# Moving the attention output's normalizing product from GpSimd to VectorE in a planned transformer block

## The chip, the cores and the metric

The kernel runs on one core of one Trainium2 chip. A core has five engines, each with its own in-order queue: TensorE (PE; its weight loads are shown apart as PEld), VectorE (DVE), ScalarE (ACT), GpSimd (POOL) and SyncE (SP), which here issues all DMA transfers. The metric is the device time of one execution in microseconds (us), as a median of runs.

## The reference

One transformer block in bf16 on 2048 tokens of width 640: a pre-norm attention with 32 heads of width 20, then a gated MLP of inner width 1728, each with a residual.

```python
h = x + _A_ref(_layernorm(x, axis=-1), A_wqkv, A_wo)
h2 = h + _B_ref(_layernorm(h, axis=-1), B_w_gate, B_w_up, B_w_down)

# _A_ref
qkv = transpose((x @ wqkv).reshape(B, S, 3, H, Dh), 2, 0, 3, 1, 4)
scores = jnp.einsum("bhqd,bhkd->bhqk", q, k) * (Dh ** -0.5)
p = _softmax(scores, axis=-1)
o = jnp.einsum("bhqk,bhkd->bhqd", p, v)
return transpose(o, 0, 2, 1, 3).reshape(B, S, D) @ wo

# _B_ref
h = gelu(x @ w_gate) * (x @ w_up)
return h @ w_down
```

## The kernel before

**Tiling.** The 2048 queries are cut into eight chunks (`SIZES` = 512, five of 256, two of 128). Heads go in eight groups of four, the four heads of a group lying at partitions 0, 32, 64 and 96. A slot is one chunk's work on as many groups as make 512 columns (a 256-query chunk has two groups per slot); there are 32 slots. Within a slot a tile is 128 x 512 scores of one head.

**Exponentials.** Score matmuls (L972) write PSUM banks 0 to 4. ACT takes them as units of alternately three and two tiles (1536 and 1024 columns) and writes bf16 weights to the ring `pts`, whose last part lies in `rege`. Some tiles (`D_SLOT`: three steps of four tiles in most slots) VectorE does instead: one instruction for each tile (L885) makes a 16-bit integer pattern from PSUM, and four value rounds of 128 x 2048 (`TERMS`, L896) turn a pattern into four bf16 terms of an exponential's approximation. Each round's result feeds its own value matmuls. `SUMS` says in how many cases of a slot two rounds are added first (a pair sum, L902), which saves PE one pass. `D_FIRST` and `D_SPAN` say over how many units of a slot these tiles are spread.

**Value matmuls and the end of a slot.** Value matmuls (L923) add up in bank 6. A column of ones in the values gives each query's sum too. When a slot is done, VectorE copies bank 6 to `osb` (L1045). For all chunks but the last `spread` (from L1019) then brings the sums, which lie in one partition for each head, to 16 columns on 128 partitions through DRAM (`sums`, then `rc`), GpSimd makes reciprocals of them with ten small instructions, and three more DMA steps (`rsums`, then four `bsum`) repeat them over 32 partitions for each head. One product, `on16 = osb * bsum`, 128 x 512 (L1034), normalizes the output, and four DMAs (`attn`) store it. When a chunk's slots are through, `post` (from L1097) runs the output projection, the second norm and the MLP of that chunk as background work beside the next chunk's slots; the norm's reciprocal root is a row of small GpSimd instructions. The last chunk's `post` is the tail.

**Order.** Nothing is ordered by hand. Every operation is given to `Sched.op` with an engine, a planned duration, a priority (lower goes first) and what it reads and writes. `schedule` plays the operations through with these durations and fixes the order of every engine's queue; `emit` writes the queues with semaphore waits. A result is taken to be ready its duration and a latency after its start: `lat`, or else the engine's entry in `DRAIN` (0.085 us for VectorE). Score matmuls are due `QK_LEAD` before ACT is expected to be free (L233). PE goes on with operations of its present tiling mode until another one has been ready for longer than `PE_AGE` (L168). Where PE would be idle too much, `schedule` puts in filler matmuls, groups of four small ones (`zer`) or one wide one on `kt_all`.

**Other names.** `XN_DVE` lists the token tiles whose transposed copy VectorE makes in the prologue, the others being ACT's. `P_EPI` is priority 2. All DMAs are issued by SP. Operations recorded through the helper `I` carry line 391 in the profile, so there the tile names tell them apart.

Of the kernel before, what the change touches and what calls it, by code (L numbers as in the profile page):

```python
# [8 lines left out]
ALU = mybir.AluOpType  # L9
# [9 lines left out]
DRAIN = {"pe": 0.165, "act": 0.115, "dve": 0.085, "pool": 0.05, "sp": 0.0}  # L19
WARM_WIN, WARM_MIN = 3.4, 0.5  # L20
PAD_WIN, PAD_MIN = 3.4, 0.42
QK_LEAD = .62
PE_AGE = 2.5
SD_AGE = 0.6


# [22 lines left out]
class Sched:  # L49
# [13 lines left out]
    def op(self, eng, fns, dur, prio, reads=(), writes=(), acq=(), rel=(), after=(), sem=None, lat=None, mode=None, util=0.0, rows=()):  # L63
        if eng == "dve" and rel and prio > self.ev:
            prio = self.ev
        o = Op()
        o.i = len(self.ops)
        o.eng, o.dur, o.lat, o.sem = eng, dur, DRAIN[eng] if lat is None else lat, sem
        o.util = util
        o.mode = mode  # L70
        o.rows = rows
        o.tag = writes[0] if writes else None
        o.fns = fns if isinstance(fns, list) else [fns]
        o.prio = (prio, o.i)
        deps = set(after)
        for r in reads:
            if r in self.lw:
                deps.add(self.lw[r])
        for w in writes:
            if w in self.lw:  # L80
                deps.add(self.lw[w])
            deps.update(self.rd.get(w, ()))
        for r in reads:
            self.rd.setdefault(r, []).append(o.i)
        for w in writes:
            self.lw[w] = o.i
            self.rd[w] = []
        deps.discard(o.i)
        o.deps = deps
        o.acq = list(acq)  # L90
        o.rel = list(rel)
        o.succ = []
        o.ready = 0.0
        self.ops.append(o)
        return o.i

    def schedule(self):
# [25 lines left out]
        while done < total:  # L123
# [4 lines left out]
            for e in ENGINES:  # L128
# [8 lines left out]
                while ready[e]:  # L137
# [28 lines left out]
                    if chosen is None:  # L166
                        chosen, banks = o, got
                        if e != "pe" or p[0] < 1 or o.mode == mode[e] or t - o.ready > PE_AGE:  # L168
                            break
# [62 lines left out]
                if e == "act":  # L232
                    due = t + o.dur + (0.905 if o.dur > 1.2 else 1.332) - QK_LEAD if o.mode == "exp" else None  # L233
                if o.util:
# [111 lines left out]
PV_QUADS = 2  # L346
PR, PR2 = 12, 4
D_SLOT = (0,) + (3,) * 27 + (2,) * 2 + (1,) * 2
SUMS = (0,) + (1,) * 30 + (0,)
HOP = 2.6  # L350
RECIP_MAGIC = float(0x7EF311C3)
COL = 256
VN = 6
SIX = ()
D_FIRST, D_SPAN = 0, 17
TANH_FROM = 768
GELU_A = 2.0 * 0.7978845608028654
GELU_B = 4.0 * GELU_A * 0.044715
# [2 lines left out]
P_EV = 1.8  # L361
P_QK, P_PV, P_TAIL, P_PRO, P_EPI, P_LN, P_BG = 0, 1, 1.2, 1.5, 2, 2.5, 3
P_KQ = 3
V_ACT = (0, 1)
XN_DVE = (13, 14, 15)
V0 = 0
LATE = (0, 1, 2, 3, 4)

# [1 line left out]
def bass_sequential_preLN__mha_block__glu_gated_geglu__prompt_kernel(  # L370
# [12 lines left out]
    with ExitStack() as es:  # L383
        sc = Sched(nc)
        op = sc.op

        def sb(name, shape, dt=BF16):
            return es.enter_context(nc.sbuf_tensor(name, shape, dt))

        def I(method, *args, **kwargs):  # L390
            return lambda eng: getattr(eng, method)(*args, **kwargs)  # L391
# [8 lines left out]
        def c_dve(n, rate=1.0625):  # L400
            return 0.061 + n * rate * 1e-3
# [23 lines left out]
        osb = sb("osb", [128, 2, 512], FP32)  # L425
        rc = sb("rc", [128, 2, 16], FP32)
        rn = sb("rn", [128, 2, 16], FP32)
        bsum = sb("bsum", [128, 512], FP32)
        on16 = sb("on16", [128, 512])
# [67 lines left out]
        def bank(b, n=512):  # L497
            return PS[:, 512 * b.b:512 * b.b + n]
# [5 lines left out]
        POOL = "pool"  # L504

        def cst(fn, key, n=128):
# [7 lines left out]
           reads=["zer"], writes=["qf1"])  # L514
        op("act", I("activation", f32(qt_all[:, 2, :, :]), zer[:, 0:2].bitcast(FP32).to_broadcast([128, 2048]), ACT.Copy), 1.8, P_QK,
           reads=["zer"], writes=["qf2"])
# [138 lines left out]
        for t0 in (0, 4, 8, 12):  # L655
# [6 lines left out]
            for t in range(t0, t0 + 4):  # L662
                e_ops.append(ln_apply("dve", x_sb[:, t, :], xn_p[:, t % 4, :], ("xnp", t % 4), t, [f"x{t // 4}"], P_PRO))
                transposes(xn_p[:, t % 4, :], [("xnp", t % 4)], xnT[:, :, t * 128:(t + 1) * 128], ("xnT", t),
                           ALLB, P_PRO, "dve" if t in XN_DVE else "act")
                e_ops.append(len(sc.ops) - 2)
# [24 lines left out]
        def dma(dst, src, key, reads, sem, lat, prio, issue=DMA_ISSUE, keep=True):  # L691
            i = op("sp", I("dma_start", dst, src), issue, prio, reads=reads, writes=[key], sem=sem, lat=lat)
            if keep:
                w_readers.append(i)
            return i
# [133 lines left out]
        for s_, (c, gs) in enumerate(slots):  # L829
            mine = list(dict.fromkeys(x[1:3] for x in tiles if x[0] == s_))  # L830
            n = D_SLOT[s_]
            d_kb[s_] = [mine[(2 * i + 1) * len(mine) // (2 * n)] for i in range(n)]
            k = min(SUMS[s_], 2 * n)
            d_sums[s_] = [(i + 1) * k // max(n, 1) - i * k // max(n, 1) for i in range(n)]
# [43 lines left out]
        def d_exp(b, tile, prio):  # L878
            c = slots[tile[0]][0]
            qb = CHUNKS[c][0] // 512  # L880
            e = min(qb, 2)
            h = len(d_raw)
            v, vk = d_v[e][d_n[e] % len(d_v[e])]
            aft = tuple(e_ops) + (tuple(last_qk[0]) if qb else ()) + (tuple(last_qk[1]) if qb > 1 else ())
            d_ops.append(op("dve", lambda eng: eng.tensor_scalar(v[:, 512 * h:512 * h + 512], bank(b), EXP_MUL, -32000.0,  # L885
                                                                 ALU.mult, ALU.max), c_dve(512), P_QK,
                            reads=[("SD", tile)], writes=[vk], rel=[b], after=aft))
            d_raw.append(tile)
            if h < 3:
                return  # L890
            d_n[e] += 1
            pairs = d_sums[tile[0]].pop(0)
            for i, off in enumerate(TERMS):
                a, ak = d_a[e][d_t[e] % len(d_a[e])]
                d_t[e] += 1
                d_ops.append(op("dve", I("tensor_scalar", a, v, 0.25, off, ALU.mult, ALU.add), 0.6, prio,  # L896
                                reads=[vk], writes=[ak], after=aft))
                if i // 2 < pairs:
                    if i % 2 == 0:
                        m, mk = a, ak  # L900
                        continue
                    d_ops.append(op("dve", I("tensor_tensor", m.bitcast(BF16), m.bitcast(BF16), a.bitcast(BF16), ALU.add), 1.13, prio,  # L902
                                    reads=[mk, ak], writes=[mk], after=aft))
                    a, ak = m, mk
                pv_op([[(a[:, 512 * k:512 * k + 512].bitcast(BF16), ak, x) for k, x in enumerate(d_raw)]], tile[0])
            d_raw.clear()
# [41 lines left out]
        def unit(u):  # L948
# [53 lines left out]
            if xd:  # L1002
                d_exp(bd, xd, P_EPI)
# [15 lines left out]
        def spread(s, c, gs, nq):  # L1019
            n = len(gs)  # L1020
            h = lambda dst, src, reads, key, sem, issue: dma(dst, src, key, reads, sem + str(s), HOP, P_EPI, issue, keep=False)
            h(sdr[s], osb[DH:128:32, s, :], [("osb", s)], ("sdr", s), "sa", 0.1)
            h(rc[:, s, :], sdr[s].rearrange("j (a b) -> (j a) b", b=16), [("sdr", s)], ("rc", s), "sb", 0.4)
            x, y, z = rc[:, s, :], rn[:, 0, :], rn[:, 1, :]
            d = lambda fn, r, w: op(POOL, fn, 0.285, P_EPI, reads=r, writes=w)
            d(I("tensor_scalar", y.bitcast(I32), x.bitcast(I32), -1.0, RECIP_MAGIC, ALU.mult, ALU.add), [("rc", s)], ["ry"])
            for i in range(3):
                d(I("tensor_tensor", z, x, y, ALU.mult), [("rc", s), "ry"], ["rz"])
                d(I("tensor_scalar", z, z, -1.0, 2.0, ALU.mult, ALU.add), ["rz"], ["rz"])
                d(I("tensor_tensor", x if i == 2 else y, y, z, ALU.mult), ["ry", "rz"], [("rc", s) if i == 2 else "ry"])  # L1030
            h(rdr[s].rearrange("j (a b) -> (j a) b", b=16), rc[:, s, :], [("rc", s)], ("rdr", s), "sc", 0.4)
            for j in range(4):
                h(bsum[32 * j:32 * j + 32, :], rdr[s, j].partition_broadcast(32), [("rdr", s)], ("bs", j), "sd", 0.36)
            op(POOL, I("tensor_tensor", on16[:], osb[:, s, :], bsum[:], ALU.mult), 1.4, P_EPI,  # L1034
               reads=[("osb", s)] + [("bs", j) for j in range(4)], writes=["on16"])
            for j in range(4):
                h(adr[c][gs[0]:gs[0] + n, j].rearrange("g e s -> e g s"),
                  on16[32 * j:32 * j + DH, :].rearrange("p (g s) -> p g s", g=n), ["on16"], ("adr", c, gs[0], j), "se", 0.36)

        def epilogue(s_, bk):  # L1040
# [6 lines left out]
            if c < len(CHUNKS) - 1:  # L1047
                spread(s, c, gs, nq)
                return
# [195 lines left out]
        for kt in range(NT):  # L1245
            proj_v(kt, 0, (6, 7), P_EPI if kt < VN else P_BG, "act" if kt in V_ACT else "dve")
        
        ui = 0
        for s_, (c, gs) in enumerate(slots):
            if c == 0:  # L1250
                g = s_
                if g + 1 in STEP:
                    t, (g0, g1) = g + 1, STEP[g + 1]
                    pr = P_EPI if t == 1 else P_KQ
                    proj_k(t, BG0, pr)
# [12 lines left out]
                if g == 7:  # L1268
# [6 lines left out]
                    for i, (dst, src, key) in enumerate(parts):  # L1275
                        ids.append(op("sp", I("dma_start", dst, src), 0.35, P_EPI, sem="wp", lat=3.4,
                                      writes=[(key, 0)], after=tuple(wr) if i < 1 else ids[-1:]))
# [42 lines left out]
```

## Time and profile before

| | us |
|---|---|
| median of 3 runs | 891.14 (890.36 to 893.83) |
| profiled execution | 892.49 |
| its span, first to last instruction | 890.8 |
| first exponential starts, last ends | 36.9, 854.9 |

| engine | idle share of the span by the page's totals | instructions |
|---|---|---|
| PE | 6% | 16553 |
| ACT | 6% | 766 |
| VectorE | 16% | 1312 |
| GpSimd | 81% | 461 |

The granted TensorE clock was 0.996 on average; two stretches of 3.4 us inside the stream of exponentials, from 258 and from 310 us, ran at half clock. DMA engines were busy for some 19% of the span.

A row of a group names line, engine, operation, tiles written and read (out<-in) with their shapes, and the count, and then busy time, mean duration in ns, and the idle time of the engine just before these instructions with what ended it. A timeline row has start and length in us; in brackets stands the idle time before it. A row of stages has the window, its length, and then busy time and count for PE, PEld, DVE, ACT and POOL, the granted clock, the DMA share and GB/s.

### The profile page before, as it was taken

To read this page: it belongs to the slowest core of one execution; us is meant where nothing else is said; L and a number is where in the kernel's file an instruction comes from. 1 tells how busy PE (TensorE), PEld (TensorE's weight loads), DVE (VectorE), ACT (ScalarE), POOL (GpSimd) and SP (SyncE) were. 2 spreads that over 40 slices of the span, in tenths; PEclk is the share of its full clock that TensorE was granted. 3 is DMA by queue.
4 is the path that set the end of the run, shared out by engine and by line. 5 is a ranking of instruction groups with operands and counts; after the bars stand their busy time and mean duration, and the time that the engine had idled before them with its cause. 6 is when DMAs were issued, how large, how long until landed. Compare 5 with 4: busy or idle time off the path is not lost.

```text
span 890.8 us, 36355 instructions
## 1 busy us (share of the span) xinstructions
PE 840.0 (94%) x16553; PEld 414.2 (47%) x16553; DVE 746.0 (84%) x1312; ACT 840.2 (94%) x766; POOL 171.5 (19%) x461
## 2 busy tenths in 40 slices
PE   3999999999989899999999999999999999999998
PEld 1532223222334344345455555555454546666676
DVE  8838998989969988788889978999899997876853
ACT  6799999999999999999999999999999999999962
POOL 5002111111111321111131321212121322121100
PEclk9999999999999999999999999999999999999999
DMA  7222120322245510001112101101110101122000
GB/s 265 78 46 58 30 71 22 88 84 66 82 116 164 147 27 17 22 4 41 41 43 56 31 20 37 34 20 34 30 53 20 24 25 44 30 36 57 12 18 16
DMA packets 57298, 46.94 MB, mean 53 GB/s; under 512 B 25524, under 2 KB 50704, under 8 KB 57144
## 3 DMA queue, kind: packets, MB, share of 16 engines
q1 hardware_dynamic: 57144, 44.62, 18.3%
q8 instruction: 129, 2.11, 1.0%
q14 instruction: 25, 0.20, 0.1%
HBM read 30.68 MB, written 11.04 MB: 47 GB/s over the span
## 4 chain that ended last, share of the span: by engine, by line
PE 44%; ACT 32%; DVE 22%; issue 1%; POOL 1%; DVEq 0%
ACT pts L391 24%; PE ps L972 13%; PE ps L391 12%; PE ps L672 10%; ACT rege L391 7%; DVE qt_all L391 6%; PE ps L677 6%; DVE rege L391 5%; DVE rege L885 3%; DVE qt_all L885 2%; PE ps L1154 1%; DVE stats L391 1%; DVE rege L1207 1%; DVE rege L1190 1%; PE ps L1219 1%
## 5 line engine op out<-in xcount | busy, mean ns | idle before, releaser
L391 ACT ACTIVATE pts<-ps 128x1024 bf16<-128x1024 f32 (+1 forms) x567 | 639.9, 1238 | 13.9 <-PE ps L972 9.4
L972 PE MATMUL ps<-qt_all,kt_all 32*128 32x256 bf16 (+2 forms) x4096 | 316.6, 273 | 13.6 <-ACT pts L391 8.4
L972 PEld LDWEIGHTS ps<-qt_all,kt_all 32*128 32x128 bf16 x4096 | 113.3, 92 | 212.2 <-ACT pts L391 99.9
L885 DVE TENSOR_SCALAR rege<-ps 128x512 int16<-128x512 f32 x216 | 147.8, 686 | 35.5 <-PE ps L972 34.0
L391 ACT ACTIVATE rege<-ps 128x1536 bf16<-128x1536 f32 x113 | 168.7, 1493 | 2.5 <-PE ps L972 2.2
L672 PE MATMUL ps<-rege,regw 128*32 128x256 bf16 (+1 forms) x3360 | 149.9, 292 | 5.2 <-ACT rege L391 1.5
L391 PE MATMUL ps<-pts,v_all 128*21 128x256 bf16 (+2 forms) x2752 | 132.8, 274 | 0.1
L391 PE MATMUL ps<-rege,v_all 128*21 128x256 bf16 (+2 forms) x1808 | 125.8, 291 | 4.0 <-DVE rege L391 3.4
L885 DVE TENSOR_SCALAR qt_all<-ps 128x512 int16<-128x512 f32 x132 | 90.5, 686 | 23.2 <-PE ps L972 22.6
L391 DVE TENSOR_SCALAR rege<-rege 128x2048 int16<-128x2048 int16 x138 | 97.8, 725 | 1.5 <-PE ps L391 0.6
L672 PEld LDWEIGHTS ps<-rege,regw 128*32 128x32 bf16 x3360 | 78.5, 96 | 39.7 <-issue 17.3
L677 PE MATMUL ps<-regw 128*128 128x512 bf16 (+1 forms) x360 | 89.7, 356 | 2.5 <-ACT regw L624 2.0
L391 POOL TENSOR_TENSOR on<-osb,bsum 128x512 bf16<-128x512 f32 x30 | 41.1, 1369 | 206.4 <-DMA bsum<-rsums 206.4
L391 PEld LDWEIGHTS ps<-pts,v_all 128*21 128x21 bf16 x2752 | 62.9, 92 | 29.2 <-issue 22.1
L391 POOL TENSOR_SCALAR rn<-rc 128x16 int32<-128x16 int32 x30 | 7.9, 264 | 355.0 <-DMA rc<-sums 354.7
L672 PE MATMUL ps<-regw,rege 128*32 128x320 bf16 x1568 | 74.9, 301 | 0.8 <-DVE rege L885 0.4
L391 DVE TENSOR_SCALAR qt_all<-qt_all 128x2048 int16<-128x2048 int16 (+3 forms) x116 | 72.3, 631 | 1.7 <-ACT qt_all L391 0.5
L391 PEld LDWEIGHTS ps<-rege,v_all 128*21 128x21 bf16 x1808 | 47.1, 91 | 45.3 <-DVE rege L391 22.4
L391 PE MATMUL ps<-qt_all,v_all 128*21 128x256 bf16 (+1 forms) x1280 | 57.4, 267 | 6.4 <-DVE qt_all L391 6.2
L391 DVE TENSOR_SCALAR qt_all<-rege 128x2048 int16<-128x2048 int16 x80 | 55.9, 714 | 0.6 <-PE ps L391 0.2
L677 PEld LDWEIGHTS ps<-regw 128*128 128x128 bf16 x360 | 29.4, 99 | 50.3 <-issue 28.1
L1207 DVE TENSOR_TENSOR rege<-rege,ps 128x512 bf16<-128x512 bf16 (+1 forms) x53 | 35.8, 676 | 13.1 <-PE ps L672 13.0
(115 smaller groups left out, 734.4 us busy)
## 6 DMA issues: line engine op xcount, KB each, us to landing
bsum<-rsums SPq DMA_DIRECT2D x120, 64.0 KB, 2.1
rege<-in_A_x_dram SPq DMA_DIRECT2D x5, 640.0 KB, 5.6
q_rows<-regw SPq DMA_DIRECT2D x20, 128.0 KB, 1.8
out_dram<-rege SPq DMA_DIRECT2D x16, 160.0 KB, 2.4
attn<-on SPq DMA_DIRECT2D x120, 20.0 KB
regw<-in_B_w_gate_dram SPq DMA_DIRECT2D x5, 432.0 KB, 3.3
regw<-in_B_w_up_dram SPq DMA_DIRECT2D x5, 432.0 KB, 3.3
kt_all<-k_rows SPq DMA_DIRECT2D x12, 160.0 KB
```

Of the source, the lines that this page charges most:

```text
L391: return lambda eng: getattr(eng, method)(*args, **kwargs)
L672: return [lambda eng, j=j: eng.matmul(out()[32 * j:32 * j + 32], l[:, 32 * j:32 * j + 32], r, start=start, stop=stop, tile_position=(0, 32 ...
L677: fn = col4(lambda: bank(bk, n), l, r, k == 0, k == len(steps) - 1) if col else lambda eng, l=l, r=r, k=k: eng.matmul(bank(bk, n), l, r, s ...
L885: d_ops.append(op("dve", lambda eng: eng.tensor_scalar(v[:, 512 * h:512 * h + 512], bank(b), EXP_MUL, -32000.0, ALU.mult, ALU.max), c_dve( ...
L972: return lambda eng: eng.matmul(out()[:, kk * nq:(kk + 1) * nq], kt_all[32 * j:32 * j + 32, g, kt * 128:(kt + 1) * 128], qt_all[32 * j:32 ...
L1154: lambda eng, a=a, f=f, fi=fi: eng.matmul(bank(bk)[:, fi * nq:(fi + 1) * nq], w[:, a, F0[f]:F0[f] + 128], hnT[:, a, 128 * tb:128 * tb + nq ...
L1190: op("dve", lambda eng, bg=bg, fv=fv, w=w: eng.tensor_scalar(fv, bank(bg, w), 0.5, None, ALU.mult), c_dve(w), p, reads=[kg], writes=hkeys( ...
L1207: hdone.append(op("dve", lambda eng, bu=bu, fv=fv, w=w: eng.tensor_tensor(fv, fv, bank(bu, w), ALU.mult), c_dve(w), p, reads=[ku] + hkeys( ...
L1219: f == NF - 1) if nq >= COL else lambda eng, f=f, o=o, hf=hf, bk=bk: eng.matmul(
```

## The change

The product of L1034 is given to VectorE, at priority `P_ON` = 2 and with VectorE's planned duration for 512 columns. The value rounds and pair sums get a planned latency of 0.3 us. Score matmuls' lead, the age at which PE changes its mode, the places of pair sums (30 before, 28 after), the spread of VectorE's tiles and one tile of the prologue's copies change too. What is computed stays.

```diff
-QK_LEAD = .62
-PE_AGE = 2.5
+QK_LEAD = .65
+PE_AGE = 3.5
...
-SUMS = (0,) + (1,) * 30 + (0,)
+SUMS = (0, 1, 1, 1, 0) + (1,) * 20 + (2, 1, 0, 1, 0, 1, 0)
 HOP = 2.6
+D_LAT = 0.3
...
-D_FIRST, D_SPAN = 0, 17
+D_FIRST, D_SPAN = 0, 16
...
+P_ON = 2
 V_ACT = (0, 1)
-XN_DVE = (13, 14, 15)
+XN_DVE = (9, 13, 15)
...
                 d_ops.append(op("dve", I("tensor_scalar", a, v, 0.25, off, ALU.mult, ALU.add), 0.6, prio,
-                                reads=[vk], writes=[ak], after=aft))
+                                reads=[vk], writes=[ak], after=aft, lat=D_LAT))
...
                     d_ops.append(op("dve", I("tensor_tensor", m.bitcast(BF16), m.bitcast(BF16), a.bitcast(BF16), ALU.add), 1.13, prio,
-                                    reads=[mk, ak], writes=[mk], after=aft))
+                                    reads=[mk, ak], writes=[mk], after=aft, lat=D_LAT))
...
-            op(POOL, I("tensor_tensor", on16[:], osb[:, s, :], bsum[:], ALU.mult), 1.4, P_EPI,
+            op("dve", I("tensor_tensor", on16[:], osb[:, s, :], bsum[:], ALU.mult), c_dve(512), P_ON,
                reads=[("osb", s)] + [("bs", j) for j in range(4)], writes=["on16"])
```

As the queues are laid out from the plan, all of them change their order. Counted over the queues, VectorE gets 30 products and loses two pair sums; GpSimd loses 30 products; PE loses 36 of 248 small filler matmuls and one of 35 wide ones, and gets two rounds of value matmuls (4 of 512 columns and 16 of 128); ACT and SP keep all their instructions.

## The prediction

> **What bounds the kernel now.** I read the page's engine totals and costliest groups first.
>
> ```profile
> PE 840.0 (94%) x16553; PEld 414.2 (47%) x16553; DVE 746.0 (84%) x1312; ACT 840.2 (94%) x766; POOL 171.5 (19%) x461
> ...
> L391 ACT ACTIVATE pts<-ps 128x1024 bf16<-128x1024 f32 (+1 forms) x567 | 639.9, 1238 | 13.9 <-PE ps L972 9.4
> ...
> L391 ACT ACTIVATE rege<-ps 128x1536 bf16<-128x1536 f32 x113 | 168.7, 1493 | 2.5 <-PE ps L972 2.2
> ...
> L391 POOL TENSOR_TENSOR on<-osb,bsum 128x512 bf16<-128x512 f32 x30 | 41.1, 1369 | 206.4 <-DMA bsum<-rsums 206.4
> ```
>
> ACT's 680 exponentials (567 + 113) fill nearly the whole span, and most of their idle time is ended by the score matmuls (L972). The view by stages of 25 us has ACT at 23.3 to 25 of every 25 us between 50 and 850. So the span has three parts: a prologue up to the first exponential (36.9 us), a stream up to the end of the last (854.9), a tail (35.9). In the stream only time that ACT loses can be won.
>
> ACT's exponentials overlap, so the idle column understates the loss. I took ACT's starts from the trace instead: after a 1024-wide exponential the next instruction normally starts 0.904 us later, after a 1536-wide one 1.331 us (medians of some 340 each). What the steps exceed these adds up to 29.7 us over the stream: 3.6 at 41 to 50 us, 26.1 later. The timeline around the longest ones:
>
> ```profile
> 255.78 1.35 POOL L391 TENSOR_TENSOR on<-osb,bsum 128x512 bf16<-128x512 f32 x1 [5.23 <-DMA bsum<-rsums]
> 256.04 2.17 DVE L391 TENSOR_TENSOR qt_all<-qt_all,rege 128x2048 bf16<-128x2048 bf16 x1
> ...
> 258.27 0.41 PE L391 MATMUL ps<-qt_all,v_all 128*21 128x256 bf16 x8 [0.76 <-DVE qt_all L391]
> ...
> 262.05 2.37 ACT L391 ACTIVATE pts<-ps 128x1536 bf16<-128x1536 f32 x2 [1.34 <-PE ps L972]
> ```
> ```profile
> 616.75 1.69 POOL L391 TENSOR_TENSOR on<-osb,bsum 128x512 bf16<-128x512 f32 x1 [10.40 <-DMA bsum<-rsums]
> ...
> 617.23 1.76 DVE L391 TENSOR_SCALAR rege<-rege 128x2048 int16<-128x2048 int16 x1
> ...
> 618.09 1.18 ACT L391 ACTIVATE pts<-ps 128x1024 bf16<-128x1024 f32 x1
> ...
> 619.05 0.40 PE L391 MATMUL ps<-rege,v_all 128*21 128x256 bf16 x8 [0.76 <-DVE rege L391]
> ...
> 619.96 2.56 ACT L391 ACTIVATE pts<-ps 128x1536 bf16<-128x1536 f32 x2 [0.68 <-PE ps L972]
> ```
>
> A GpSimd product (`on`) starts; the VectorE instruction that meets it takes 2.17 us where its like takes 1.22, or 1.76 where it takes 0.69; the value matmuls that need its result hold PE's queue for 0.76 us; the score matmuls behind them come late; ACT waits. In the second place ACT's step is 619.96 - 618.09 = 1.87 us, 0.96 too long. In the first the loss is larger, since PE, starved (busy 0.88 of 2 us from 256 to 258), then runs at half clock:
>
> ```profile
> 260.00:262.00 2.00, 2.00 (x28) 0.85 (x20) 0.00 (x0) 0.70 (x1) 0.00 (x0) 0.51 0.09 26
> ```
>
> **The change, part by part.**
>
> *The product leaves GpSimd.* I went through all 30. In 18 a VectorE instruction that overlaps it is lengthened by 0.14 to 1.08 us, 14.3 us in all: pattern rounds from SBUF, gelu and norm steps, one pair sum. Instructions that read PSUM are not lengthened. In the 7 us from each of these 18, ACT loses 13.3 us (0.74 each); after the other 12 it loses 1.2 us (0.10 each). What the collisions cost is 18 x (0.74 - 0.10) = 11.5 us. With the product off GpSimd they are gone: **-11.5**. Bounds: -13.3, and -6 if something else ends the same waits half of the time.
>
> *The product comes to VectorE.* 30 instructions, two f32 operands in SBUF, bf16 out: not in the trace. Nearest by size and f32 type is the output copy from PSUM:
>
> ```profile
> L391 DVE COPY osb<-ps 128x512 f32<-128x512 f32 x32 | 21.9, 686 | 6.2 <-PE ps L391 6.2
> ```
>
> Below it lies the bf16 tensor_tensor of that size (420 ns), above it the pair sum of 2048 (1217 ns). I take 0.69: 30 x 0.69 = 20.6 us of VectorE, against 14.3 of stretch and two pair sums (2 x 1.22) given back, so +3.9 on an engine that is busy 746 of 891. On ACT's path it costs less, as the order is laid out with it: stretches of around the product's length (0.48 to 0.76 us, seven of the 18), which no order foresaw, cost ACT 0.49 us each, 0.39 above the 0.10 of undisturbed windows. So the bounds are 0 and 30 x 0.39 = 11.7. A VectorE instruction that the order foresees is nearer to the undisturbed windows (by 1312 in 891 us their seven us hold some ten of them, and lose 0.10 in all): **+2.0**.
>
> *Its wait moves with it.* On GpSimd the product waited 206 us for the sums' way through DRAM and held up nothing. On VectorE everything behind it would wait: pattern rounds, then value matmuls, then scores. From the copy `osb` to the product's start the trace shows 11.2 to 20.7 us, median 15.5. In the new order 22 to 35 VectorE instructions stand between the two (14 for the last), 15.1 to 22.1 us of work by their durations in the trace (9.5 for the last); divided by VectorE's 84% that is 18.0 to 26.3 (11.4). Two or three products are tight, the last most of all (18.5 us before; its VectorE there also waited for PE). **+0.5**, bounds 0 and the rival below. The four `attn` issues behind each product keep their place relative to it on SP.
>
> *Later value matmuls (D_LAT, 0.085 to 0.3), QK_LEAD, PE_AGE, D_SPAN.* They move instructions on PE; none is added. They aim at the waits of value matmuls for rounds (PE's weight loads, 23.0 us for `rege` and 17.6 for `qt_all`), most of them off ACT's path. The 29.7 less 13.3 and 3.6 leaves 12.8 us of losses, none above 0.4 us, for them to win or enlarge. **-1.0**, bounds -4 and +2: a third of those won, a sixth added.
>
> *Fewer fillers and pair sums.* PE loses 36 filler matmuls (248 to 212; four take some 0.2 us, 2 us in all) and one wide one, and gains two rounds of value matmuls (two times 0.2). Hidden under ACT: 0.
>
> *Prologue.* One transposed tile's copy goes from ACT to VectorE, another back; matmuls ahead of the first scores stay 150. 0, bounds +-1.
>
> *Tail.* PE, the tail's bound, has 581 matmuls behind its last scores before, 533 after: 56 fewer of 32x320, 7 more of 128x128, one filler.
>
> ```profile
> 857.58 3.70 PE L672 MATMUL ps<-regw,rege 128*32 128x320 bf16 x104
> ...
> 867.41 3.07 PE L1154 MATMUL ps<-rege,regw 128*128 128x128 bf16 x52
> ```
>
> 56 x 3.70/104 = 2.0 less, 7 x 3.07/52 = 0.4 and about 0.3 more: **-1.3**, bounds -2.5 (the norm's chain gets shorter too) and +1.
>
> Sum: -11.5 + 2.0 + 0.5 - 1.0 - 1.3 = -11.3. The profiled execution took 892.49 us (span 890.8 and 1.7 around it), 1.35 above the median of 891.14. So 881.2 on its scale, 879.8 on the median's: **880**.
>
> A rule speaks against the change. The Trainium skill ("SBUF — State Buffer", Who interferes with whom) says that GpSimd and VectorE share one pair of ports as an exclusive lock, and that a VectorE instruction with two SBUF inputs, as the moved product is, is blocked by a GpSimd instruction that reads SBUF. The first timeline agrees: 256.04 + 2.17 = 258.21 is GpSimd's end, 257.13, and nearly the sum's own 1.22. By that rule the product would now meet the reciprocal steps that GpSimd keeps; the last rival prices this.
>
> **The rivals.**
>
> *PE takes over.* PE is busy 94%. If it can give back only half of ACT's losses, the removal is worth 5.8 and the rest is as above: 891.1 - 5.6 = 885.5. For: in the stages of the stream PE is at 23 to 25 of 25 us. Against: its weight loads wait 99.9 us for ACT to free the banks.
>
> *Displacement.* The products cost VectorE what unforeseen stretches cost: +11.7 in place of +2.0, so 889.5. For: from 575 to 600 and 675 to 700 VectorE is busy 25.0 of 25. Against: undisturbed windows.
>
> *VectorE waits for the sums (slower).* Each us of late VectorE cost 11.5/14.3 = 0.8 us of ACT. With -11.3 otherwise, the kernel is slower by over 0.5% (895.6) from (11.3 + 4.5)/0.8 = 20 us of such waits, 0.66 per product over the slack counted above; at 1 us each it is 879.8 + 24 = 904. For: single in-order queue, landings up to 20.7 us. Against: most products have 3 us of slack or more.
>
> *Half clock.* Fewer fillers let PE's granted clock fall more often. The two falls in the stream (258 and 310 us) lost ACT 2.0 and 1.7 us, both behind a collision. Four more: 887.
>
> *GpSimd's small instructions block the product.* Ten of 0.26 to 0.33 us each per slot and the norm's. One per product: 30 x 0.33 x 0.8 = 8, so 888. Against: 97 pattern rounds that overlapped small GpSimd instructions took 694 ns on average, 687 without.
>
> **How the numbers follow.** Forecast 0.60, PE 0.13, displacement 0.11, waits 0.08, small instructions 0.05, half clock 0.03. This measurement can tell about 0.5% from no change: 886.7 and 895.6. The forecast and most of PE and of half clock lie below (0.75); displacement, small instructions and the rest of PE between (0.17); waits above (0.08). The range: low end 880 with the product at nothing (-2), the losses' third (-3) and the tail (-1.2): 873. High end 890, with displacement in it and the waits left out.
>
> **What would show it.** No VectorE instruction lengthened beyond 0.1 us by GpSimd; the 2048-wide rounds all near 0.69; ACT's losses at 15 to 20 us in the stream in place of 29.7; the product at 0.69 with little idle time before it ended by `bsum`; the tail about 1 us shorter. It is wrong if ACT's idle time ended by L972 stays, or if VectorE shows long waits for `bsum`.

## The result and the profile after

The changed kernel took 888.97 us (median of 18 runs, 886.13 to 895.07), the kernel before 893.77 us beside it: a ratio of 0.9949, 95% interval 0.9927 to 0.9971. Two repeats (chips 13 and 15) gave 0.9913 (0.9883 to 0.9944) and 0.9928 (0.9897 to 0.9958). The mean of the three is 0.9930, or 6.2 us of 891; the forecast was 11.3. So the change is faster, by about half of what was predicted (4.5 us in the first comparison alone).

The engine totals of the changed kernel and the groups that answer to those of before:

```profile
span 886.2 us, 36314 instructions
...
PE 839.1 (95%) x16536; PEld 416.4 (47%) x16536; DVE 746.2 (84%) x1340; ACT 838.5 (95%) x766; POOL 131.8 (15%) x431
...
L393 ACT ACTIVATE pts<-ps 128x1024 bf16<-128x1024 f32 (+1 forms) x567 | 642.8, 1255 | 13.1 <-PE ps L974 8.1
...
L393 ACT ACTIVATE rege<-ps 128x1536 bf16<-128x1536 f32 x113 | 170.9, 1512 | 1.5 <-PE ps L974 0.9
```

ACT's idle column hardly moved (13.9 + 2.5 before, 13.1 + 1.5 here). The losses counted from ACT's starts, as in the prediction, show more: 29.7 us before, 26.9 here. Of the span, the prologue has 35.7 us, the stream 815.3, the tail 35.2; before these were 36.9, 818.0 and 35.9. The prologue lay between 35.6 and 36.6 in other runs with the changed kernel's order, and between 35.7 and 36.9 with the old one, so its difference is not shown to be an effect of the change.

The groups by shape show that both halves of the mechanism came as forecast. First a group of value rounds before, then the same group after, with the product:

```profile
L391 DVE TENSOR_SCALAR rege<-rege 128x2048 int16<-128x2048 int16 x138 | 97.8, 725 | 1.5 <-PE ps L391 0.6
```
```profile
L393 DVE TENSOR_SCALAR rege<-rege 128x2048 int16<-128x2048 int16 x138 | 92.6, 686 | 1.5 <-PE ps L393 0.6
...
L393 DVE TENSOR_TENSOR on<-osb,bsum 128x512 bf16<-128x512 f32 x30 | 20.5, 682 | 4.0 <-DMA bsum<-rsums 4.0
```

The rounds fell from 725 to 686 ns, in the stream only one VectorE instruction is still lengthened by GpSimd by over 0.1 us (a pattern round at 250.9 us, by 0.36, beside a GpSimd memset), and the product takes 0.68 us. The last column is new: VectorE waits 4.0 us for `bsum`, in three places. Where the longest wait falls (8th product), the timeline of the changed kernel reads:

```profile
258.60 0.69 DVE L393 TENSOR_TENSOR on<-osb,bsum 128x512 bf16<-128x512 f32 x1 [2.17 <-DMA bsum<-rsums]
259.21 0.69 DVE L393 TENSOR_SCALAR rege<-rege 128x2048 int16<-128x2048 int16 x1
...
259.95 0.61 PE L393 MATMUL ps<-rege,v_all 128*21 128x256 bf16 x8 [2.17 <-DVE rege L393]
...
261.58 1.45 ACT L393 ACTIVATE pts<-ps 128x1536 bf16<-128x1536 f32 x1 [2.58 <-PE ps L974]
```

It is the chain that the prediction described for a collision, with another head: the product waits, the round behind it is late by as much, PE's value matmuls wait 2.17 us for the round, and the scores behind these come late for ACT. The stages of 2 us (window, length, then PE, PEld, VectorE, ACT, GpSimd, granted clock, DMA share, GB/s) add one more link:

```profile
258.00:260.00 2.00, 0.05 (x4) 0.05 (x8) 1.40 (x3) 1.00 (x2) 0.00 (x0) 0.91 0.73 221
260.00:262.00 2.00, 2.00 (x32) 0.78 (x36) 0.88 (x2) 0.42 (x1) 0.00 (x0) 0.50 0.30 65
```

PE does next to nothing for 2 us (busy 0.05) and is then granted half the clock. In the 7 us behind this one product ACT loses 3.3 us, behind the 30th 1.4, behind the other 28 together 3.7.

### The profile page after: what moved, and what is told of

Same layout as the page of the kernel before. It is cut to its first block, busy times and chain, and to the rows that moved or that the text cites. A ratio compares the mean times of both kernels' runs of the same rounds, so it can differ in the third digit from the quotient of the medians.

```text
span 886.2 us, 36314 instructions
## 1 busy us (share of the span) xinstructions
PE 839.1 (95%) x16536; PEld 416.4 (47%) x16536; DVE 746.2 (84%) x1340; ACT 838.5 (95%) x766; POOL 131.8 (15%) x431
## 4 chain that ended last, share of the span: by engine, by line
ACT 47%; PE 41%; DVE 8%; DMA 2%; issue 1%; SPq 1%; DVEq 0%
ACT pts L393 35%; PE ps L974 13%; ACT rege L393 11%; PE ps L674 11%; PE ps L393 10%; PE ps L679 5%; PE ps L1156 1%; DVE rege L393 1%; DVE rege L887 1%; DVE stats L393 1%; PE ps L1221 1%; ACT qt_all L393 1%; DMA bsum<-rsums 1%; SPq L393 1%; DVE qt_all L393 1%
## 5 line engine op out<-in xcount | busy, mean ns | idle before, releaser
L393 ACT ACTIVATE pts<-ps 128x1024 bf16<-128x1024 f32 (+1 forms) x567 | 642.8, 1255 | 13.1 <-PE ps L974 8.1
L974 PE MATMUL ps<-qt_all,kt_all 32*128 32x256 bf16 (+2 forms) x4096 | 320.3, 273 | 15.5 <-ACT pts L393 8.8
L974 PEld LDWEIGHTS ps<-qt_all,kt_all 32*128 32x128 bf16 x4096 | 115.9, 92 | 217.1 <-ACT pts L393 110.9
L393 ACT ACTIVATE rege<-ps 128x1536 bf16<-128x1536 f32 x113 | 170.9, 1512 | 1.5 <-PE ps L974 0.9
L393 DVE TENSOR_SCALAR rege<-rege 128x2048 int16<-128x2048 int16 x138 | 92.6, 686 | 1.5 <-PE ps L393 0.6
L679 PE MATMUL ps<-regw 128*128 128x512 bf16 (+1 forms) x360 | 87.8, 352 | 2.9 <-ACT regw L626 2.0
L393 DVE TENSOR_SCALAR qt_all<-qt_all 128x2048 int16<-128x2048 int16 (+3 forms) x116 | 68.2, 597 | 1.5 <-PE ps L393 0.7
L393 PEld LDWEIGHTS ps<-rege,v_all 128*21 128x21 bf16 x1828 | 48.3, 91 | 40.4 <-issue 20.3
L674 PEld LDWEIGHTS ps<-regw,rege 128*32 128x32 bf16 x1568 | 36.1, 96 | 21.2 <-issue 10.4
```

The lines of the kernel that those rows point to most:

```text
L674: return [lambda eng, j=j: eng.matmul(out()[32 * j:32 * j + 32], l[:, 32 * j:32 * j + 32], r, start=start, stop=stop, tile_position=(0, 32 ...
L679: fn = col4(lambda: bank(bk, n), l, r, k == 0, k == len(steps) - 1) if col else lambda eng, l=l, r=r, k=k: eng.matmul(bank(bk, n), l, r, s ...
L974: return lambda eng: eng.matmul(out()[:, kk * nq:(kk + 1) * nq], kt_all[32 * j:32 * j + 32, g, kt * 128:(kt + 1) * 128], qt_all[32 * j:32 ...
```

## The experiments

Ratios are to the kernel before on the same chip, in five rounds where nothing else is said. "Loss" is ACT's loss in the stream counted from its starts.

### Engine and order apart

The change has two parts: which engine makes the product, and the order of all queues. `e1` takes the new order and hands the product back to GpSimd after the order is fixed; `e2` takes the old order and puts the product on VectorE at the place where it was planned for GpSimd.

```diff
         sc.schedule()
+        for i in prods:
+            sc.ops[i].eng = POOL    # e1, on the changed kernel; "dve" in e2, on the kernel before
```

> The changed kernel's order on every queue, but the product is emitted on GpSimd again; nothing else moves. Collision theory: VectorE instructions are lengthened by the product again, by 0.5 to 1.1 us in half or more of the slots, and ACT's losses in the stream (26.9 us in the changed kernel) rise by 8 to 11 us, less some 4.5 us for the two waits of VectorE for bsum (258 and 811 us) that go with the product: 4 to 7 us slower than the changed kernel. Rival, that the collisions only marked places where the old order lost time anyway: ACT's losses fall by the two waits, 3 to 4 us faster than the changed kernel.

> The old kernel's order on every queue, but the product is emitted on VectorE, where the plan had it start on GpSimd; the plan left no room for it there. Collision theory with the forecast's small price of the product: 7 to 10 us faster than before (11.5 for the collisions, less 2 to 4). If the product costs as much there as an unforeseen stretch (0.39 us each, 11.7): no change. If VectorE's waits for bsum count for most of it: some of the 30 products show waits of 1 us and more, and the time is that of before or worse.

Measured: `e1` 1.0012 (0.9995 to 1.0030), loss 31.3 us; `e2` 0.9995 (0.9981 to 1.0010), loss 28.4. Neither part alone gains anything. The new order does not avoid the collisions: in `e1` the product lengthens 18 VectorE instructions again, by 11.3 us in all. And in the old order a product that no plan foresees costs on VectorE what it cost on GpSimd: ACT loses 0.45 us in the 7 us behind each of `e2`'s products (0.49 in the kernel before), where VectorE waits only 2.85 us in all for `bsum`. The displacement rival is true in the old order.

`e4` asks whether those products stand too early: each goes another five VectorE instructions later, with the stores behind it.

```diff
+        for i in prods:
+            sc.ops[i].eng = "dve"
+            sc.move(i, 5)
```

> As the previous old-order kernel, with each product another five VectorE instructions later, so that bsum has landed. No wait for bsum is left, and the difference to the kernel with the products at their early place is the price of such waits; what is left against before is the collisions' 11.5 us less the product's own displacement: 8 us faster by the forecast, 0 by the displacement rival.

Measured: 1.0042 (1.0022 to 1.0062). No product waits for `bsum` any more, and still ACT loses 0.51 us behind each, so it is not the wait that they cost. That it is slower than `e2` as well (loss 34.5 against 28.4) is for the larger part a fall of the clock: in its profile the granted clock is halved for 10.2 us from 119.7 us, and 3.7 of the 6.1 us lie between 86 and 136 us. `e2`'s profile has no fall in the stream, and only four of `e4`'s twelve runs (892.5 to 893.8 us) show a full clock. What set it off was not tested.

### Each term by itself

Three runs in the same rounds on one chip put a price on the terms: two variants and the changed kernel. In `e11` (old order, GpSimd) and `e12` (new order, VectorE) the product is cut to 16 of its 512 columns in 29 of the 30 slots; the rest of the normalization is left out.

```diff
         sc.schedule()
+        for s, i in prods[1:]:
+            sc.ops[i].fns = [I("tensor_tensor", on16[:, 0:16], osb[:, s, 0:16], bsum[:, 0:16], ALU.mult)]
```

> Order of before, product still on GpSimd, but in 29 of the 30 slots it is cut to 16 of its 512 columns: the rest of the normalization is left out. Nothing else moves, so this measures the term of 11.5 us that the prediction put on the collisions, by itself. The prediction's theory: no lengthened VectorE instructions, ACT's loss in the 7 us behind the products falls from 14.8 us to about 4, and the kernel is 9 to 13 us faster than before (ratio 0.986 to 0.990). Rival, the collisions end waits that something else would end a little later: 3 to 6 us faster (0.993 to 0.997).

> Order of the changed kernel, product on VectorE, but in 29 of the 30 slots cut to 16 columns: the rest of the normalization is left out. The waits for bsum stay, the 0.69 us of each product go. The prediction's price of a product that the order foresees (2.0 us in all): 1 to 4 us faster than the changed kernel on this chip. Rival, displacement at its full price of 0.39 us for each product: 9 to 12 us faster.

> The changed kernel as it is, beside the three others on the same chip: 0.991 to 0.995 of before.

Measured: `e11` 0.9883 (0.9857 to 0.9908), `e12` 0.9900 (0.9876 to 0.9924), the changed kernel beside them 0.9928. In `e11` the groups show what is gone:

```profile
L391 DVE TENSOR_SCALAR rege<-rege 128x2048 int16<-128x2048 int16 x138 | 93.4, 693 | 1.5 <-PE ps L391 0.6
L391 POOL TENSOR_TENSOR on<-osb,bsum 128x16 bf16<-128x16 f32 x29 | 9.4, 323 | 194.8 <-DMA bsum<-rsums 194.8
```

The product takes 0.32 us in place of 1.37, the rounds are back at 693 ns, and the loss is 20.4 us. In the 7 us behind the products ACT loses 5.7 us, where the two profiles of before have 14.8 and 13.8. So the collisions cost 0.0117 x 891 = 10.4 us (8.2 to 12.7), as the prediction's theory had it. `e12` against the changed kernel's mean gives the product's length where the order foresees it: (0.9930 - 0.9900) x 891 = 2.7 us, or 0.09 each. `e2` against `e11` gives it where nothing does: (0.9995 - 0.9883) x 891 = 10.0 us, or 0.33 each. (The cut product still takes 0.16 us on VectorE, so the first of these prices is that of the missing 0.52.)

### The wait of the 8th product

Why is `bsum` late there? The view of SP's queue in the changed kernel, and then in the kernel before, at the same slot:

```profile
250.77 0.36 SPq L393 DMA_DIRECT2D regw<-in_B_w_gate_dram  x1
251.17 0.58 SPq L393 DMA_DIRECT2D qt_all<-bounds  x1
251.80 0.56 SPq L393 DMA_DIRECT2D regw<-in_B_w_down_dram  x1
252.40 3.38 SPq L393 DMA_DIRECT2D bsum<-rsums  x4
```
```profile
242.78 1.51 SPq L391 DMA_DIRECT2D qt_all<-q_rows  x4
...
249.46 0.35 SPq L391 DMA_DIRECT2D regw<-in_B_w_gate_dram  x1
...
250.49 0.55 SPq L391 DMA_DIRECT2D regw<-in_B_w_down_dram  x1
251.09 2.97 SPq L391 DMA_DIRECT2D bsum<-rsums  x4
```

Two weight loads of the MLP stand ahead of the four `bsum` steps in SP's in-order queue. From the copy `osb` to the landing of `bsum` it took 20.0 us here; the median of the 30 is 15.0. The loads alone don't explain it, as they stand ahead of `bsum` in the old order too, where the same way took 16.1 us. What differs is their company: the four `qt_all<-q_rows` loads, which the old order issues at 242.78 us, come from 247.06 to 248.57 us in the new one, right in front of the weight loads. The first `bsum` step is then issued 13.9 us after `sums` in place of 11.5, and the steps take longer to land, as the DMA view has it (before, 241 to 257 us; then after, 246 to 259 us; the last number is the median time from issue to landing in us):

```profile
bsum<-rsums SPq DMA_DIRECT2D x4, 64.0 KB, 2.7
```
```profile
bsum<-rsums SPq DMA_DIRECT2D x4, 64.0 KB, 4.1
```

The first trial, `e3`, moved the two worst products (8th and 30th, with their stores) four VectorE instructions later. The second, `e9`, left VectorE alone and issued the two loads behind `bsum` in that slot.

```diff
+        for i in (7, 29):
+            sc.move(prods[i], 4)                  # e3
...
+        sc.sums_first(7, ("wp", "wd2"))           # e9: these two semaphores' loads go behind the 4th bsum
```

> The changed kernel's order, with only the two products that wait 2.17 and 1.46 us for bsum (8th and 30th) put four VectorE instructions later, their stores with them. If these waits cost what the trace suggests, ACT's losses after 258 us fall from 3.2 to under 0.5 us and those after 811 us by about 1 us: 3.5 to 4.5 us faster than the changed kernel. Rival, that PE would have been late there anyway: under 1 us.

> The changed kernel's order, except that in the 8th slot the two weight loads that stand ahead of bsum on SP's queue are issued behind it. If they make bsum late, the 8th product's wait of 2.17 us falls below 0.5 us and ACT's loss behind it from 3.3 to under 0.7 us: 2 to 3 us faster than the changed kernel. Rival, that the transfers themselves are slow there: the wait stays above 1.5 us. Second rival, that the loss moves on to the next slots: the wait goes, and the time stays within 1 us.

> The changed kernel once more, for a second profiled execution: how much of what its first profile shows stays. If the waits for bsum at the 8th and 30th product come from the order, they are there again with 1.5 to 2.5 us and ACT loses 4 to 5 us behind them; if they are chance, they move to other products. The span of its parts should agree within 1 us each.

> The order with the two weight loads behind bsum in the 8th slot once more, now beside the changed kernel in the same rounds. If the 2.2 us wait of the 8th product is the mis-sized term, 2 to 5 us faster than the changed kernel (ratio lower by 0.002 to 0.006). If the first comparison was the luck of one chip: within 1 us of it.

> The changed order with the two weight loads behind bsum, a third time. If the wait of the 8th product costs 2 to 5 us: 0.988 to 0.991 of before. If not: 0.992 to 0.994, as the changed kernel.

`e3`: 0.9942 (0.9922 to 0.9962), no gain that can be told. The 8th product no longer waits, but the 9th and 10th do, for 1.62 and 2.56 us, and ACT loses 1.9 and 2.4 behind them: the wait moved on to the next slots, which the expectation had not foreseen.

`e9`: SP's queue and the tile view of the product, with the time that VectorE sat idle before it:

```profile
251.71 2.45 SPq L407 DMA_DIRECT2D bsum<-rsums  x4
254.20 0.42 SPq L407 DMA_DIRECT2D regw<-in_B_w_gate_dram  x1
254.67 0.56 SPq L407 DMA_DIRECT2D regw<-in_B_w_down_dram  x1
```
```profile
L407 DVE TENSOR_TENSOR on<-osb,bsum x30: 673/682/693, 88.8 to 807.5; 128x512 bf16<-128x512 f32 x30
its engine sat idle before it (us, times) until:
  DMA bsum<-rsums: 1.5, 3
```

The way of the sums is 16.7 us in that slot (16.9 and 16.7 in the repeats), the `bsum` steps land in 2.6 us, and in all three profiles of `e9` the 8th product finds its data there. In the two repeats of the changed kernel, with the loads ahead, it waits again: 2.63 and 2.21 us, with 3.3 and 2.8 us lost by ACT behind it. (The 30th product's wait of 1.46 us shrank to 0.83 and 0.47 there.) The stage where the changed kernel had half the clock, in `e9`:

```profile
258.00:260.00 2.00, 2.00 (x46) 0.96 (x46) 1.33 (x3) 2.00 (x3) 0.00 (x0) 1.00 0.84 233
260.00:262.00 2.00, 1.68 (x33) 0.47 (x25) 1.24 (x3) 2.00 (x3) 0.00 (x0) 1.00 0.24 77
```

The loss is 21.7, 24.9 and 21.6 us (mean 22.7) against 26.9, 26.0 and 23.1 in the three profiles of the changed kernel (25.3). The times are less clear: 0.9899 (0.9878 to 0.9921), 0.9927 (0.9899 to 0.9954) and 0.9919 (0.9898 to 0.9939), on average 0.9915, 1.3 us below the changed kernel's 0.9930. Where both ran in the same five rounds (the second of these three) they were equal. That the wait is gone is shown; that the whole kernel is faster for it is likely, but not separated from nothing. All three are faster than the kernel before.

`e13` is `e9` with the product cut as in `e12`: the new order without the 8th product's wait and without most of the product. Waits of 1.7 us for `bsum` stay, in four other places.

> Order of the changed kernel, product on VectorE and in 29 of the 30 slots cut to 16 columns (the rest of the normalization is left out), and the two weight loads of the 8th slot issued behind bsum. Against the old order without collisions (e11_no_collisions: 0.9883 of before, 20.4 us lost in the stream) this shows the new order by itself, without the product's length and without the 8th product's wait. If that wait is what made the new order no gain (e12_small_product: 0.9900), about 0.987 and 21 us lost. If the rest of the order is the dearer part, about 0.990 again.

Measured: 0.9894 (0.9873 to 0.9916), loss 21.0 us, stream 808.7 and tail 35.3 us. `e11`, the old order in the same condition, had 0.9883, 20.4, 808.2 and 35.7. By itself the new order shows no gain: +1.0 us by the times (with both intervals, some 3 either way), +0.1 us by stream and tail.

### What the planner does with it

Five more runs let the planner make a new order after one edit. `e5` is the kernel before with nothing but the product given to VectorE (`c_dve(512)`, priority `P_EPI`); the others are the changed kernel with one line changed: `e6` plans the product on GpSimd (1.4 us, `P_EPI`), `e7` plans the landing of `bsum` 2 us later, `e8` sets `D_LAT` back, `e10` plans the weight loads at 5.0 us in place of 3.4.

```diff
-D_LAT = 0.3
+D_LAT = DRAIN["dve"]                                          # e8
...
-... dma(dst, src, key, reads, sem + str(s), HOP, P_EPI, ...)
+... dma(dst, src, key, reads, sem + str(s), HOP + 2.0 * (sem == "sd"), P_EPI, ...)   # e7
...
-... sem="wp", lat=3.4,
+... sem="wp", lat=5.0,                                        # e10
```

> The old kernel with the product alone given to VectorE at its planned duration; all constants as before, the order planned anew. If what pays is that the order foresees the product, the 7 us after the products lose ACT 3 to 6 us in all in place of 14.8, and the kernel is 4 to 8 us faster than before. If the other constants are needed for the gain, 0 to 2 us faster, with VectorE's waits for bsum or other losses of ACT in the profile.

> The changed kernel with the product planned and emitted on GpSimd as before; all other constants as in the change. If the product's move is the gain, collisions as before (13 to 15 us lost after the products) and the time within 2 us of before. If the later value matmuls and the moved pair sums gain something by themselves, 2 to 4 us faster than before, and ACT's losses away from the products below the 14.9 us of before.

> The changed kernel with bsum planned to land 2.0 us later, the order planned anew, so that VectorE reaches the products later. If the waits for bsum (4.0 us in the changed kernel, two of them losing ACT 4.7 us) took the missing gain, no wait above 0.3 us is left, and it is 2 to 5 us faster than the changed kernel. Rival, that the waits move on as the stores behind the products come later on SP's queue too: waits of 1 us and more appear elsewhere between 250 and 330 us, and the time is that of the changed kernel within 1.5 us.

> The changed kernel with the value rounds' planned latency back at 0.085 us. If the later value matmuls help, PE's weight loads wait again some 40 us for rounds (17 in the changed kernel) and it is 1 to 4 us slower than the changed kernel. If these waits are off ACT's path: within 1.5 us.

> The changed kernel with each weight load planned to take 5.0 us in place of 3.4, so that SP's queue is not laid out to wait for one ahead of the sums' way; planned anew, with the same PE work behind the last scores (29.4 us). If the late bsum is what kept the change from its full gain, no product waits over 0.5 us and it is 3 to 5 us faster than the changed kernel; if a newly planned order loses as much elsewhere, within 1.5 us of it or slower.

| run | ratio (95%) | loss in the stream | tail |
|---|---|---|---|
| `e5` product only | 1.0071 (1.0053 to 1.0089) | 30.3 | 41.8 |
| `e6` product planned on GpSimd | 1.0025 (1.0006 to 1.0044) | 28.2 | 40.1 |
| `e7` landing 2 us later | 1.0007 (0.9988 to 1.0027) | 30.1 | 38.3 |
| `e8` `D_LAT` back | 1.0009 (0.9994 to 1.0024) | 24.6 | 44.7 |
| `e10` weights 5.0 us | 0.9936 (0.9913 to 0.9959) | 25.4 | 35.3 |

`e5` shows that a foreseen product is cheap with the old constants too: only 5.6 us are lost behind its products in place of 14.8, and yet the kernel is 6 us slower than before. The tail is the largest part of what `e5`, `e6` and `e8` lose against the changed kernel (4.8 to 9.5 us longer). The windows of the tail, in the changed kernel and in `e8`:

```profile
851.00:886.20 35.20, 30.27 (x506) 25.43 (x502) 18.75 (x44) 11.21 (x15) 0.00 (x0) 1.00 0.06 20
```
```profile
846.80:891.40 44.60, 40.35 (x812) 34.31 (x800) 25.40 (x60) 12.52 (x17) 0.00 (x0) 1.00 0.05 17
```

PE has 40.4 us of work behind the last exponential in place of 30.3, 812 matmul records in place of 506. In the stream `e8` loses no more than the changed kernel (24.6 us; 26.9, 26.0 and 23.1 in the latter's three profiles), though PE's weight loads wait 24.3 us for value rounds in place of 17.0; it has left background work for the end. So the constants that were tried are not shown to act by what they are named for: each draws another plan, and the plan of the diff is one with a short tail. (`QK_LEAD`, `PE_AGE`, `SUMS` and `D_SPAN` were not tried one by one.) `e7` also took the waits down (one of 1.27 us left) and `e10` cut the 8th's to 0.83 us; neither is faster than the changed kernel. `e7` has a stream and a tail that are each 3 to 4 us longer; `e10` loses 2.1 us at 319 us, where a load lands late and the clock falls.

A second profile of the kernel before, unchanged:

> The old kernel once more, for a second profiled execution: 13 to 16 us lost by ACT in the 7 us after the products, as in its first profile, if the collisions come from the order.

One profile, 889.65 us, loss 27.5 us, of which 13.8 lie behind the products (14.8 in the first), with no fall of the clock at 260 or 310 us; the profile that the prediction was made from had both. Profiles of one order differ by 2 to 4 us in such places, so a single one can't settle terms of that size.

## Why the prediction was right in its direction and too large

The runs can be joined to a chain from the kernel before to the changed one. Each measured number is the difference of two ratios times 891 us:

| step | runs | predicted | measured |
|---|---|---|---|
| collisions gone | before to `e11` | -11.5 | -10.4 |
| later value matmuls, tail, prologue (new order) | `e11` to `e13` | -2.3 | +1.0 |
| the product's length on VectorE | `e13` to `e9`, mean of three | +2.0 | +1.9 |
| its waits for `bsum` | `e9` to changed, means of three | +0.5 | +1.3 |
| sum | | -11.3 | -6.2 |

Each step carries some 2 to 3 us of uncertainty; the first is far above it, the others are not. Three of the runs stood in the same rounds on one chip, and there the picture is sharper: before to `e11` -10.4, `e11` to `e12` (the new order with all its waits) +1.5, `e12` to the changed kernel (the product) +2.5. For the middle step the prediction had -1.0 - 1.3 + 0.5 = -1.8. The six times of `e11` lie between 881.1 and 882.2 us, those of `e12` between 881.9 and 884.4 (difference of the means 1.4 us, 95% interval 0.7 to 2.2), so that the new order gave back time in place of gaining it is clear of noise; some tenths of it may be the 0.16 us that each cut product takes on VectorE.

The prediction also named what would show it wrong, and both signs came: ACT's idle time ended by score matmuls stayed (11.6 us before, 9.0 after), and VectorE showed a long wait for `bsum`.

*The product leaves GpSimd* was right in mechanism and size. Counting ACT's loss behind each disturbed product against the undisturbed ones gave 11.5, and removing the overlap alone gave 10.4.

*The product comes to VectorE* was right too, with its reason: 2.0 against 1.9, by the other pair of runs (changed kernel and `e12`) 2.7. The upper bound of 11.7, for a product that no order foresees, was nearly met by `e2`: 10.0. The displacement rival was thus wrong for this kernel because its order foresees the product, and right for the other order.

*Later value matmuls* (-1.0) and *Tail* (-1.3) are the steps that failed: by the table they are the largest share of the difference, 3.3 of 5.1 us. The waits of value matmuls for rounds, which the later value matmuls aim at, did shrink: PE's weight loads wait 29.3 us for `rege` and `qt_all` in `e11` and 12.0 in `e13`. But the stream did not get shorter by it (808.2 and 808.7 us), so these waits were off ACT's path, as the prediction itself thought of most of them. From 436 to 736 us the loss is a little smaller (4.6 us in `e13`, 5.1 in `e11`), but in the two stretches of 100 us from 336 and from 736 us it is 1.1 larger together. The tail got 0.4 to 0.7 us shorter, not 1.3: the matmuls that left it are as many as counted (PE's busy time in it fell from 31.6 to 30.3 us), but PE's idle time there grew from 4.3 to 4.9, and half of the gain went into it. The -1.0 was a third of the small losses, taken with no row that showed it; zero was the value that the evidence bore.

*Its wait moves with it* (+0.5) was undersized. I expected two or three products to be tight, and three wait: the 8th 2.17, the 26th 0.34, the 30th 1.46 us. Two things were wrong in the step. The room between copy and product was given as 18.0 to 26.3 us by dividing the work in it by VectorE's average share of 84%; in the trace it is mostly 17 to 18, because VectorE is busier there (90% in the median) than on average. (For the last product 11.4 was given and 17.7 found.) And I compared that room with landings of the old order, though SP's queue had been reordered too: the 8th `bsum`, which landed 16.1 us after its copy in the old order, took 20.0 in the new one, behind the weight loads and the four loads of `qt_all` that now come just ahead of these. At the prediction's own rate of 0.8 us of ACT per us of late VectorE, 4.0 us of waits are 3.2; the trace of the first profile shows 4.7 behind the two long ones, since the clock fell behind one of them. The times give 1.3 (all waits of the 8th product removed), so the price lies between these.

*Fewer fillers* at nothing, and the *half clock* rival: PE's granted clock is 0.998 in the three profiles of the changed kernel, and 0.996 and 1.000 in the two of before. Each of the three profiles of the changed kernel has its fall at 260 to 264 us, behind the 8th product's wait, and `e9` and `e13`, with as few fillers, have none there; so it goes with the wait and not with the fillers. *PE takes over* would have left ACT's losses after the removal; in `e11` they fell to 20.4 us, so PE did not keep the gain. *GpSimd's small instructions* did not block the product: 671 to 693 ns over all 30, of which only one met any. The forecast that ACT's losses would come to 15 to 20 us was wrong (26.9, 26.0 and 23.1): even with neither collision nor product `e11` has 20.4, of which 3.1 is one step at 46 us that no variant touched.

The first comparison (-4.5 us) is also the least favourable of three; the repeats gave 7.8 and 6.4. The steps above are set against their mean.

## What to carry to other kernels

An operation that is moved to a busier engine is paid by what the order knows of it: the same 30 instructions cost 10 us where they were dropped into a finished order and 2 to 3 where the order was laid out with them. When an operation that waits for a DMA moves into a queue that matters, look at the landing in the new order of the issuing queue, and at which transfers stand ahead of it there and run beside it, not at the landings of before. And where a planner lays out everything anew, price the edit by runs at a fixed order and the plan by its tail; of small gains that no row shows, count none.

## What the runs showed of the hardware

A wait on VectorE cost more than its length where PE ran dry: 2.17 us of wait, 2 us without a matmul, then a granted clock of 0.50 from 260 to 262 us, and 3.3 us lost on ACT. The same fall came from a wait of another kind in the second run of `e9`. The timeline and the stage behind it:

```profile
314.15 1.32 PE L688 MATMUL ps<-rege,regw 128*32 128x512 bf16 x20 [1.93 <-DMA rege<-xn_t]
```
```profile
316.00:318.00 2.00, 2.00 (x38) 0.92 (x38) 1.79 (x4) 1.88 (x2) 1.13 (x4) 0.50 0.02 1
```

Here a transposing load landed late, PE stood for 1.93 us, and ran at half the clock from 316 to 318 us; ACT lost 3.5 us. In the two other profiles of the same order ACT loses 0.3 us at this place and the clock stays at 1.00. In one profile of the changed kernel (`after_again`) PE stood there for 1.69 us: ACT lost 2.2 us, and the clock did not fall. So a late landing of some 2 us is one reason why runs of one order differ by 3 us.

When GpSimd and VectorE meet, which of them waits was left open in the prediction. In the changed kernel one product meets small GpSimd instructions (timeline):

```profile
456.17 0.19 POOL L393 TENSOR_SCALAR rs<-nw 128x2 int32<-128x2 int32 x1
...
456.96 0.68 DVE L393 TENSOR_TENSOR on<-osb,bsum 128x512 bf16<-128x512 f32 x1
457.17 0.52 POOL L393 TENSOR_TENSOR nw<-nw 128x2 f32<-128x2 f32 x1
```

The GpSimd instruction (`nw`) that began inside the product ends with it (457.17 + 0.52 = 457.69; 456.96 + 0.68 = 457.64) and takes 0.52 us where its like alone takes 0.2; the product keeps its 0.68. In the kernel before it was the VectorE instruction that began inside a GpSimd product and ended after it. So the later one pays. Both agree with the Trainium skill ("SBUF — State Buffer", Who interferes with whom), by which the order of issue decides who blocks.
